# Splitting the masked queries of a two-stage attention kernel in three pieces of 512 columns in place of one of 1536

## The chip, the core and the metric

The kernel runs on one core of one Trainium2 chip. The metric is the time of one execution on the device in microseconds (us), the median of several runs. The engines are named as the profile names them: PE (TensorE, matmuls), PEld (its weight loads), DVE (VectorE), ACT (ScalarE), POOL (GpSimd) and SP (SyncE, which issues every DMA here).

## The reference

Two stages follow each other, for 8 batches `b`. In the first, 512 tokens and 32 state rows of 8 heads read each other by attention; this gives 576 rows of 512 columns. The second is a mixture of 4 attention experts of width 64, with 2 experts chosen for each token:

```python
logits = x @ w_gate                      # top 2 of 4 experts, softmax over the two: w
for e in range(E):
    q, k, v = x @ wq[e], x @ wk[e], x @ wv[e]
    scores = where(causal, -1e9, scale * (q @ k.T))
    ye = softmax(scores) @ v @ wo[e]
    out += (w of e where e was chosen) * ye
```

## The kernel before

**Numbers in two parts.** Matrix products run in f16, and an f32 operand is carried as a high part (rounded to f16) and a low part (what the rounding left). A product of two such operands is three matmuls: high by high, high by low, low by high (`PROD`). `split(n, hi, lo, src)` makes both parts of an f32 tile of n columns in two instructions. The high part is a copy that may run on ACT, POOL or DVE; the low part is the subtraction `src - hi`, which may run on POOL or DVE.

**The stages.** For each batch, `front(b)` loads x, splits it (`xh`, through the scaled copy `xn`), transposes it (`xT`), does the first stage's attention (`eb`, `at`), projects to keys (`kt`), values (`v`) and queries, and routes the tokens (`gate`). Then `probs(b, i)` and `reads(b, i)` run over 4 blocks `i` of 128 queries: scores, exponentials (`p`), their split (`ph`), a transposing DMA (`pt`), the product with the values (`z`), the output product and its store. Every second batch, `tail` does the state rows of two batches. `side` computes the state's reading of the tokens.

**The masked queries.** Only two of a token's four experts count, so the queries are folded: `projected(0, pr)` gives the queries of the expert pair `pr` in PSUM, and `mt[:, k]`, of three planes k of 512 columns, holds which tokens use which expert. Four DVE products write `qf` (f32, 128 x 3 x 512, one buffer): the first pair writes plane 0 and one half of plane 1 (64 partitions), the second pair plane 2 and the other half of plane 1. Plane 1 is therefore complete only with the last of the four, planes 0 and 2 before it. `split` then makes `qm` (f16, 128 x 2 x 3 x 512, two buffers), high and low. `probs` of every block reads all of `qm`: first planes 2 and 0 in all three products, high parts first, then the mask, then plane 1.

**The order of the work.** The kernel writes no order by hand. `Steps` collects every step with its duration, the views that it reads and writes and the engines that may run it (`either`), and derives from overlapping views which step waits for which. `plan` then places the steps one after the other, each at the engine where it would end first, with a bias against some engines: from batch 1 on `LEAN` adds 2.0 to DVE and 0.3 to ACT and POOL; for batch 0 `LEAN0` adds 0.3 to DVE and nothing to the others. It makes a DVE operation that shares POOL's access to SBUF (two SBUF inputs, for one) wait for POOL's current one. `run` repeats this over several rounds and then over 100 random changes of the steps' due times, and emits the best order that it has seen by its own estimate. All compute instructions are issued in one line, L447 of the profile, so groups are told apart by tiles.

Of the kernel before, what the change touches and what calls it, by code (L numbers as in the profile page):

```python
# [451 lines left out]
def state_read_then_moe_attention(ctx: ExitStack, tc: tile.TileContext, x, state, w_gate, wq, wk, wv, wo, out):  # L452
# [9 lines left out]
    B, H, S, D = x.shape  # L462
# [36 lines left out]
    def dve(n, f, **kw):  # L499
        st.do("DVE", 0.065 + n * 0.00104, f, **kw)  # L500
# [4 lines left out]
    def split(n, hi, lo, src):  # L505

        st.either([("ACT", 0.093 + n * 0.000833, (nc.scalar.activation, dict(out=hi, in_=src, func=AF.Copy, scale=1.0))),
                   ("POOL", 0.162 + n * 0.000832, (nc.gpsimd.tensor_scalar, dict(out=hi, in0=src, scalar1=1.0, scalar2=1.0, op0=ALU.mult, op1=ALU.mult))),
                   ("DVE", 0.065 + n * 0.00065, (nc.vector.tensor_copy, dict(out=hi, in_=src)))])
        kw = dict(out=lo, in0=src, in1=hi, op=ALU.subtract)  # L510
        st.either([("POOL", 0.147 + n * 0.001887, (nc.gpsimd.tensor_tensor, kw)), ("DVE", 0.065 + n * 0.00104, (nc.vector.tensor_tensor, kw))])
# [170 lines left out]
    def front(b):  # L682
# [126 lines left out]
        qm = st.buf("qm", [P, 2, 3, S], F16, bufs=2)  # L809
# [31 lines left out]
        qf = st.buf("qf", [P, 3, S], F32, bufs=CFG["qf"])  # L841
        for pr, h in (0, slice(D, P)), (1, slice(0, D)):
            pp = projected(0, pr)
            for r, k in (slice(0, P), 2 * pr), (h, 1):
                dve(S, nc.vector.tensor_tensor, out=qf[r, k], in0=pp[r], in1=mt[r, k], op=ALU.mult)
        split(3 * S, qm[:, 0].rearrange("p k s -> p (k s)"), qm[:, 1].rearrange("p k s -> p (k s)"), qf.rearrange("p k s -> p (k s)"))
        base = st.base
        st.stream("side", base + CFG["SIDE"], PACE * CFG["FSPAN"], 4.0)
        if b < CFG["PX"]:
# [276 lines left out]
    for b in range(B):  # L1126
        st.stream("front", (b - CFG["FRONT"]) * PACE, PACE * CFG["FSPAN"], 18.0)
        load(b, marks.get("w") if CFG["LB"] == 2 else None)
        front(b)
        st.stream("main", b * PACE, PACE, 16.0)  # L1130

        blocks = range(T) if b < B - 1 else range(T - 1, -1, -1)
        for k in range(T + LAG):
            if k < T:
                probs(b, blocks[k])
            if k >= LAG:
                reads(b, blocks[k - LAG])
        if b % NB == NB - 1:
            st.stream("tail", (b + CFG["TOFF"]) * PACE, PACE * CFG["TSPAN"], 8.0)
            tail(b // NB)  # L1140
# [29 lines left out]
```

## Time and profile before

| | us |
|---|---|
| time of 3 runs: median (lowest to highest) | 338.25 (337.67 to 338.3) |
| the profiled execution's own time | 337.99 |
| its span, first to last instruction | 336.2 |
| PE busy | 302.5 (90%) |
| DVE busy | 252.5 (75%) |
| POOL busy | 249.5 (74%) |
| ACT busy | 217.0 (65%) |

The span begins 0 at the first instruction. A row of a timeline gives start, duration, engine, operation, tiles and, in brackets, the idle time just before it and what ended it.

### The profile page before, as it was taken

Reading aid. Unit: us, or ns where it says so; the run is one execution under the profiler, and the core shown is the slowest. Engines: PE = TensorE matmul, PEld = TensorE weight load, DVE = VectorE, ACT = ScalarE, POOL = GpSimd, SP = SyncE. Lnnn points to the kernel's source line nnn. Section 1 sums busy time; section 2 is a strip of 40 time slices with the busy share of each in tenths; the row PEclk is TensorE's granted clock in tenths of the full one; section 3 lists DMA queues with packets and bytes.
Section 4 is the critical chain, followed back from the end, with each engine's and each line's share of the span. In section 5 each row is a group of like instructions: output and inputs, shape, how many; then the busy total and the mean of one; then the engine's idle time right before and its main releaser. Section 6 shows DMA issues by size and latency. Waiting matters only on the chain.

```text
span 336.2 us, 8884 instructions
## 1 busy us (share of the span) xinstructions
PE 302.5 (90%) x3274; PEld 198.5 (59%) x3274; DVE 252.5 (75%) x813; ACT 217.0 (65%) x481; POOL 249.5 (74%) x315
## 2 busy tenths in 40 slices
PE   6678698798897999999997999989999999999992
PEld 5445474584544776576664765467555876666750
DVE  4889969999988775998678656897679667775430
ACT  4686786585656975596688268665684867555431
POOL 8089497398988799999977999965996484485500
PEclk9999979999999899999999999999999999999998
DMA  8939649736788939989999795599696533357963
GB/s 195 216 98 204 169 96 183 164 62 121 104 171 111 208 80 189 190 192 201 195 169 168 162 202 96 79 179 167 137 154 128 111 64 69 72 97 133 142 155 98
DMA packets 142851, 48.16 MB, mean 143 GB/s; under 512 B 121816, under 2 KB 138200, under 8 KB 142808
## 3 DMA queue, kind: packets, MB, share of 16 engines
q1 hardware_dynamic: 142808, 47.61, 75.5%
q8 instruction: 25, 0.41, 0.5%
q14 instruction: 18, 0.15, 0.2%
HBM read 11.54 MB, written 8.91 MB: 61 GB/s over the span
## 4 chain that ended last, share of the span: by engine, by line
PE 37%; DVE 18%; POOL 15%; DMA 12%; ACT 11%; issue 5%; SPq 1%; ACTq 0%; POOLq 0%; DVEq 0%
PE bank L447 37%; DMA xn<-in_x_dram 3%; DMA pt<-ph 3%; POOL ph L447 3%; POOL xh L447 3%; DVE sbm L447 2%; DVE eb L447 2%; DVE m L447 2%; ACT e L447 2%; POOL at L447 2%; DVE qf L447 1%; DMA xT<-xh 1%; DMA p<-in_moe_wo_dram 1%; SPq L447 1%; POOL xn L447 1%
## 5 line engine op out<-in xcount | busy, mean ns | idle before, releaser
L447 PE MATMUL bank<-kt,qm 64*128 64x128 f16 (+7 forms) x384 | 50.0, 300 | 3.0 <-ACT p L447 1.4
L447 POOL TENSOR_TENSOR ph<-p,ph 128x256 f16<-128x256 f32 (+3 forms) x30 | 41.4, 1382 | 9.7 <-ACT ph L447 9.4
L447 PE MATMUL bank<-wo_n,z 128*128 128x512 f16 x192 | 47.0, 386 | 0.3 <-DMA z<-zh 0.3
L447 PE MATMUL bank<-v,pt 128*128 128x193 f16 x480 | 45.6, 249 | 0.7 <-DMA pt<-ph 0.7
L447 PE MATMUL bank<-at,gs 128*128 128x512 f16 x192 | 44.8, 380 | 0.5 <-DVE mx L447 0.5
L447 PEld LDWEIGHTS <-pt 128*128 128x128 f16 x480 | 40.9, 99 | 5.9 <-DMA pt<-ph 1.2
L447 ACT ACTIVATE p<-bank,mx 128x128 f32<-128x128 f32 (+3 forms) x64 | 31.5, 525 | 17.8 <-DVE mx L447 15.7
L447 POOL TENSOR_TENSOR xh<-xn,xh 128x512 f16<-128x512 f32 x28 | 33.8, 1207 | 2.3
L447 DVE TENSOR_REDUCE mx<-bank 128x1 f32<-128x128 f32 (+3 forms) x64 | 28.8, 480 | 8.7 <-PE bank L447 8.6
L447 ACT ACTIVATE o<-bank 128x512 f32<-128x512 f32 x34 | 20.2, 595 | 22.7 <-PE bank L447 22.7
L447 PE MATMUL bank<-gs,at 128*128 128x256 f16 (+1 forms) x384 | 31.2, 221 | 1.8 <-DVE at L447 1.0
L447 PEld LDWEIGHTS <-qm 64*128 64x128 f16 (+1 forms) x384 | 21.9, 96 | 18.4 <-issue 3.8
L447 PEld LDWEIGHTS <-z 128*128 128x128 f16 x192 | 17.8, 98 | 21.0 <-issue 2.6
L447 PEld LDWEIGHTS <-gs 128*128 128x128 f16 x192 | 17.5, 97 | 21.4 <-issue 3.1
L447 POOL TENSOR_TENSOR qm<-qf,qm 128x1536 f16<-128x1536 f32 x7 | 21.7, 3104 | 10.7 <-ACT qm L447 10.6
L447 PEld LDWEIGHTS <-at 128*128 128x128 f16 x384 | 24.1, 97 | 8.2 <-issue 1.9
L447 POOL TENSOR_TENSOR eb<-eb,sbm 128x512 f32<-128x512 f32 x16 | 16.7, 1049 | 12.8 <-DVE sbm L447 8.9
L447 DVE TENSOR_TENSOR qf<-bank,mt 128x512 f32<-128x512 f32 (+1 forms) x32 | 21.3, 683 | 3.6 <-ACT mt L447 1.7
L447 ACT ACTIVATE ph<-p 128x512 f16<-128x512 f32 (+3 forms) x28 | 21.1, 753 | 4.2 <-DMA pt<-ph 3.9
L447 ACT ACTIVATE xh<-xn 128x512 f16<-128x512 f32 x32 | 18.9, 625 | 5.7 <-DMA xn<-in_x_dram 4.9
L447 DVE SCALAR_TENSOR_TENSOR v<-bank,v 128x256 f16<-128x256 f32 x32 | 13.2, 420 | 10.2 <-ACT v L447 10.2
L447 PEld LDWEIGHTS <-bd 128*64 128x64 f16 x264 | 14.0, 109 | 11.4 <-issue 4.1
(170 smaller groups left out, 698.8 us busy)
## 6 DMA issues: line engine op xcount, KB each, us to landing
xn<-in_x_dram SPq DMA_DIRECT2D x16, 512.0 KB, 4.7
out_dram<-o SPq DMA_DIRECT2D x64, 128.0 KB, 2.5
sn<-in_state_dram SPq DMA_DIRECT2D x6, 128.0 KB, 2.8
p<-in_moe_wo_dram SPq DMA_DIRECT2D x2, 256.0 KB, 4.8
pt<-ph SPq DMA_TRANSPOSE x32, 4.0
out_dram<-o SPq DMA_DIRECT2D x2, 256.0 KB
z<-zh SPq DMA_TRANSPOSE x29, 2.9
xT<-xh SPq DMA_TRANSPOSE x28, 3.9
```

The lines of the kernel that those rows point to most:

```text
L447: f(**{k: v.ap() if isinstance(v, View) else v for k, v in kw.items()})
```

## The change

One call of `split` on all 1536 columns of `qf` becomes three calls on 512 columns, one for each plane k. So each batch has three high steps and three low steps, each of which waits only for the DVE products that write its plane, and each of which the planner may give to another engine. All else in the source is the same, and the planner makes the whole order anew.

```diff
-        split(3 * S, qm[:, 0].rearrange("p k s -> p (k s)"), qm[:, 1].rearrange("p k s -> p (k s)"), qf.rearrange("p k s -> p (k s)"))
+        for k in 0, 1, 2:
+            split(S, qm[:, 0, k], qm[:, 1, k], qf[:, k])
```

## Rows read from the trace of the kernel before

**Rows 1.** Busy us by stretch; columns: length, PE, PEld, DVE, ACT, POOL, clock, DMA, GB/s
```profile
40.00:50.00 10.00, 7.92 (x121) 6.40 (x121) 6.86 (x19) 8.94 (x19) 9.51 (x12) 0.83 0.37 76
50.00:60.00 10.00, 8.31 (x83) 4.55 (x82) 9.18 (x30) 6.61 (x17) 6.89 (x7) 1.00 1.05 177
60.00:70.00 10.00, 7.52 (x97) 4.88 (x94) 9.74 (x24) 5.98 (x14) 5.05 (x6) 1.00 0.55 120
70.00:80.00 10.00, 9.68 (x143) 8.05 (x141) 9.71 (x37) 7.56 (x18) 9.75 (x10) 1.00 0.70 134
80.00:90.00 10.00, 7.21 (x70) 3.50 (x69) 9.87 (x29) 5.82 (x15) 8.31 (x11) 1.00 0.48 92
...
107.00:137.00 30.00, 29.79 (x336) 20.84 (x337) 21.68 (x80) 23.12 (x55) 27.36 (x34) 0.94 0.80 160
...
245.00:310.00 65.00, 64.75 (x727) 43.08 (x728) 47.75 (x166) 41.97 (x91) 42.33 (x45) 1.00 0.54 104
```

**Rows 2.** Instructions of the tile qm: nanoseconds min/median/max, first and last start
```profile
L447 ACT ACTIVATE qm<-qf x7: 1467/1482/1484, 48.1 to 288.7; 128x1536 f16<-128x1536 f32 x7
L447 POOL TENSOR_TENSOR qm<-qf,qm x7: 3097/3106/3109, 75.5 to 290.3; 128x1536 f16<-128x1536 f32 x7
L447 DVE TENSOR_TENSOR qm<-qf,qm x1: 1949/1949/1949, 49.6 to 49.6; 128x1536 f16<-128x1536 f32 x1
L447 POOL TENSOR_SCALAR qm<-qf x1: 1464/1464/1464, 195.2 to 195.2; 128x1536 f16<-128x1536 f32 x1
```

**Rows 3.** Timeline of batch 0, 44 to 52 us
```profile
44.77 2.73 DVE L447 TENSOR_TENSOR qf<-bank,mt 128x512 f32<-128x512 f32 x4 [1.70 <-ACT mt L447]
...
48.06 1.48 ACT L447 ACTIVATE qm<-qf 128x1536 f16<-128x1536 f32 x1
48.17 1.16 POOL L447 TENSOR_TENSOR xh<-xn,xh 128x512 f16<-128x512 f32 x1
...
49.57 1.95 DVE L447 TENSOR_TENSOR qm<-qf,qm 128x1536 f16<-128x1536 f32 x1 [1.20 <-ACT qm L447]
...
50.00 2.54 POOL L447 TENSOR_TENSOR xh<-xn,xh 128x512 f16<-128x512 f32 x1
...
51.57 0.29 PE L447 MATMUL bank<-kt,qm 128*128 128x128 f16 x2 [1.21 <-DVE qm L447]
```

**Rows 4.** Timeline of batch 1, 71 to 79 us
```profile
71.43 2.01 DVE L447 TENSOR_TENSOR qf<-bank,mt 64x512 f32<-64x512 f32 x3
...
75.50 3.10 POOL L447 TENSOR_TENSOR qm<-qf,qm 128x1536 f16<-128x1536 f32 x1
...
78.66 0.28 PE L447 MATMUL bank<-kt,qm 128*128 128x128 f16 x2 [0.33 <-POOL qm L447]
```

**Rows 5.** Timeline of batch 2: its last part and its first score product
```profile
113.89 3.11 POOL L447 TENSOR_TENSOR qm<-qf,qm 128x1536 f16<-128x1536 f32 x1 [1.05 <-ACT qm L447]
...
119.14 0.51 PE L447 MATMUL bank<-kt,qm 128*128 128x128 f16 x6
```

**Rows 6.** Groups by shape: count, busy us, mean ns, idle before
```profile
L447 POOL TENSOR_TENSOR a<-e,a 128x512 f16<-128x512 f32 x14 | 16.2, 1156 | 1.2
L447 POOL TENSOR_SCALAR xn<-xn 128x512 f32<-128x512 f32 x28 | 18.7, 667 | 0.1
L447 DVE TENSOR_TENSOR ph<-p,ph 128x512 f16<-128x512 f32 x1 | 0.7, 693 | 0.4 <-ACT ph L447 0.4
L447 ACT ACTIVATE xh<-xn 128x512 f16<-128x512 f32 x32 | 18.9, 625 | 5.7 <-DMA xn<-in_x_dram 4.9 <-PE bank L447 0.7
```

**Rows 7.** Chain that ended last, around 195 us
```profile
194.34 0.87 POOL z L447 x2
195.21 1.45 POOL qm L447
...
198.18 4.29 DMA xn<-in_x_dram
```

**Rows 8.** Timeline, 145 to 147 us: a POOL and a DVE operation
```profile
145.83 1.05 POOL L447 TENSOR_TENSOR eb<-eb,sbm 128x512 f32<-128x512 f32 x1
145.94 0.96 DVE L447 TENSOR_SCALAR s<-s 128x2 f32<-128x2 f32 x1
```

**Rows 9.** Groups by shape: DVE's reciprocal of the two columns of s
```profile
L447 DVE RECIPROCAL s<-s 128x2 f32<-128x2 f32 x8 | 1.2, 156 | 0.1
```

**Rows 10.** Waits of all engines: who waited for whom, us, times, longest
```profile
PE bank L447 <- DVE xt_tail L447: 2.5, 1, 2.5
```

## The prediction

> **What bounds the kernel now.** I read the busy shares of the whole span first, then busy time by stretch, because an average over 336 us hides which engine is short where. Four stretches matter [rows 1]. From 107 to 137 us and from 245 to 310 PE is busy 29.79 of 30 and 64.75 of 65 us: nothing that makes an operand ready sooner can shorten these unless PE reaches them sooner. From 50 to 90 us it is DVE that is full: 9.18, 9.74, 9.71 and 9.87 of each 10 us, together 38.50 of 40, while PE does 8.31 + 7.52 + 9.68 + 7.21 = 32.72, so it idles 7.28. Between 40 and 50 POOL (9.51) and ACT (8.94) are the full ones. So time can be won ahead of 90 us, in the first two batches; what is won there is kept only if the nearly full engines behind it keep up, and POOL with 27.36 of 30 us from 107 on is the one to watch.
>
> Next I read the tile of the change. Each of the 8 batches has one high part of 1.48 us (7 on ACT, one on POOL of 1.46) and one low part (7 on POOL of 3.11, one on DVE of 1.95) [rows 2]. Then the timelines around them, to see how long PE stands for them. In batch 0 it waits 1.21 us for the DVE low part [rows 3], in batch 1 0.33 us for POOL's [rows 4]. In the others it doesn't: in batch 2 the low part ends at 113.89 + 3.11 = 117.00 and the first score product starts at 119.14 [rows 5], and none of the five later ones shows a wait of PE for qm.
>
> **The change part by part.** *Instructions and busy time.* Two instructions of 1536 columns become six of 512. ACT's copy of 512 columns costs 0.625, POOL's subtraction 1.156, DVE's 0.693, POOL's one-input operation 0.667 [rows 6]. Three of a kind against one: ACT 3 x 0.625 - 1.48 = +0.40, POOL's low part 3 x 1.156 - 3.11 = +0.36, DVE's 3 x 0.693 - 1.95 = +0.13, POOL's high part 3 x 0.667 - 1.46 = +0.54. With the engines of now that is 7 x 0.40 + 0.54 = 3.3 us of high parts and 7 x 0.36 + 0.13 = 2.7 us of low parts over the whole span. Nearly all of it falls where ACT or DVE have room; if all were on the path it would cost 6.0 us.
>
> The Trainium skill speaks on both sides here. Its page Perfetto Trace Analysis, section Optimizing Scalar/DVE Operations, says that each ScalarE or VectorE operation carries a fixed access overhead, so that larger operations pay on a saturated engine, and also that breaking up instructions may let work finish sooner where these engines are not saturated but leave bubbles on others. The rows agree with the first half as far as a fixed cost goes (+0.40 us on ACT). By the first half alone the time would rise by up to the 6.0 us; by the second, batch 0 gains. The sum below doesn't use the page.
>
> *Batch 0.* The four qf products run from 44.77 to 47.50. The one high part starts only at 48.06 and ends at 49.54; DVE stands 1.20 us for it, then makes the low part until 51.52; PE goes on at 51.57 after 1.21 us of idling [rows 3]. With three steps, plane 0 can be copied after the first product, and planes 0 and 2 need not wait for the last. DVE's 1.20 us of standing go, since the first low part needs a high part of 0.63 and not of 1.48 us, and two of these could be done before 48.06. DVE is the engine that is full for the next 40 us, so I count these 1.20 us as won. PE's own 1.21 us lie behind the same wait and are not counted a second time. Bounds: nothing, if ACT, full here, takes the copies no sooner than 48.06 and each low part waits for a free POOL; at most 47.50 + 0.63 + 0.69 = 48.82 in place of 51.52, 2.7 us. I take 1.2, what the rows call idle.
>
> *Batch 1.* The last qf product ends at 73.44, and the low part at 78.60, of which 3.10 are POOL's [rows 4]. Three pieces could end near 73.44 + 0.63 + 1.16 = 75.2, 3.4 us sooner, but PE waited only 0.33 us, with the key-side products filling the rest. I take 0.3; bounds 0 and 0.8, as DVE is full and sets when the next operands come.
>
> *Batches 2 to 7.* No wait of PE is removed, so no gain. The loss is on POOL. In the chain that ended last POOL runs almost alone around 195 us; the high part of batch 4 is in it with 1.45 us, ahead of the load of xn that the chain waits for next [rows 7]. If high and low stayed on POOL, this place would cost 0.54 + 0.36 = 0.9 us more. The planner can send single pieces to ACT or DVE, which it could not do with parts of one, so I take half, 0.4; bounds 0 and 0.9. The four other low parts, and the stores and loads that SP issues, I cost at nothing: PE's full queue covers them (64.75 of 65 us); without that cover they cost 0.36 us each.
>
> *Sum.* On the profiled execution: 337.99 - 1.2 - 0.3 + 0.4 = 336.9 us. The median of the runs is 338.25, 0.26 above that execution, so the forecast for a median is 337.15, rounded 337.1, 0.3% faster. A measurement of this kernel can tell about 0.2%, 0.7 us, from no change. By the bounds, all gains and no loss give 338.25 - 2.7 - 0.8 = 334.75; no gain and the loss of batch 4 give 339.15.
>
> **The rivals.** *The three DVE pieces wait three times for POOL (slower).* The trace shows that the two engines hold each other up. DVE's low part runs from 49.57 to 51.52, and POOL's xh, which starts at 50.00 and takes 1.16 us elsewhere, takes 2.54 [rows 3]. The other way round, DVE's scaling of two columns starts at 145.94 beside a POOL operation that ends at 146.88 and itself ends at 146.90, 0.96 us after its start [rows 8], where another operation on the same two columns takes 0.156 [rows 9]. In batch 0 POOL is busy without a break. One low part on DVE meets it once; three meet it up to three times. With 1.16 us for a POOL operation that has just begun and half of it, 0.58, on average, two further meetings cost 1.2 us, 2.3 at worst, on the engine that is full to 90 us. If that happens in batch 0 and again in batch 1, where a piece may go to DVE now, 2.4 us are lost on average and the gain of 1.5 is gone too, or partly: 338.25 + 2.4 - 0.5 = 340.2. It decides as soon as two or more pieces of the first batches are on DVE beside a POOL with no gaps. Against it: from batch 1 on the planner's bias of 2.0 keeps DVE from most pieces. The Trainium skill has this as a rule: its page SBUF — State Buffer, section SBUF: two separate sides, describes one port pair that DVE and GpSimd take in turn for a whole instruction, the other being blocked. Rows 3 and 8 agree with it.
>
> *The new order loses more than the pieces win (slower).* Every step is placed anew, and the search stops after a fixed number of rounds. What one badly placed step costs can be read from the waits: PE once stands 2.5 us for a low part of xt_tail [rows 10]. A second such wait ahead of a stretch in which PE is full, less the gain of 1.1, gives 338.25 + 2.5 - 1.1 = 339.65. For it speaks that PE has no slack to make it good after 107 us; against it, that a new order may as well lose the wait of now, which is the same 2.5 us the other way and part of why the range reaches below the sum.
>
> *Nothing comes of it (same).* DVE is full for 40 us behind batch 0. If the 1.20 us that it stood are filled with work that must then be done anyway, but PE's next operands still come at the old times, for instance because x arrives by DMA, the gain ends at 90 us: 338.25, at most 0.7 either way.
>
> **How the numbers follow.** The forecast (faster, most likely 337.1) has a chance of 0.43, with an own range from 334.8 to 337.5; nothing 0.19; three waits for POOL 0.20; the new order 0.18. Faster by over 0.2% is 0.43, within 0.2% 0.19, slower by over 0.2% 0.38. Cases of both signs are likely, so the range takes in both: down to 334.7 by the bounds, and up to 341.0, which is the first rival with its worst price in one batch and its average in the other, 338.25 + 2.3 + 1.2 - 0.5 = 341.25, cut slightly to leave out no more than 2 in 10 in all.
>
> **What would show it.** Right: ACT copies of 512 columns inside the run of the qf products in batch 0; DVE idle before its first low part under 0.3 us in place of 1.20; the first score product of batch 0 ahead of 51 us by a microsecond or more; PE idle between 40 and 90 us below the 2.08 + 7.28 us of now; and the later PE-full stretches as long as before but shifted forward. Wrong by the first rival: DVE low pieces of clearly more than 0.69 us, or POOL operations of 2 us beside them, before 90 us. Wrong by the second: a PE wait of 2 us or more that is not in the old list, on a tile that has nothing to do with the queries. Wrong by the third: batch 0 ahead, and the stretch that begins at 107 us where it was.

## The result, and the profile after

The changed kernel takes 333.84 us in the median (332.95 to 338.3, 4 runs; 332.95 to 334.33 without the highest) beside 337.96 of the kernel before (337.38 to 338.3): ratio 0.9872, 95% interval 0.9845 to 0.9898. Two later measurements gave 334.25 beside 337.24 (0.9925, 0.9883 to 0.9967) and 334.15 beside 337.52 (0.9889, 0.9852 to 0.9926). So it is faster by 0.8 to 1.3%, 3 to 4 us, where 1.1 us had been forecast, and the time lies just below the forecast range. One execution says less than I had assumed: 12 of the kernel before, timed beside the first of these later measurements, spread from 334.45 to 338.95 us.

The profile shown is of a second run of the changed kernel (334.44 us, span 332.2), because the first one that was taken (338.3 us) was disturbed. Busy time by stretch, columns as in [rows 1]:

```profile
40.00:50.00 10.00, 9.06 (x126) 6.31 (x125) 8.83 (x26) 8.91 (x22) 8.13 (x10) 1.00 0.31 28
50.00:60.00 10.00, 9.56 (x82) 5.29 (x81) 9.14 (x26) 7.81 (x17) 9.67 (x11) 1.00 1.03 158
60.00:70.00 10.00, 9.49 (x170) 7.69 (x168) 9.14 (x29) 5.67 (x16) 7.17 (x10) 1.00 1.14 204
70.00:80.00 10.00, 8.79 (x99) 6.57 (x97) 8.50 (x33) 6.91 (x18) 8.16 (x9) 1.00 0.96 171
80.00:90.00 10.00, 8.57 (x73) 4.57 (x73) 9.24 (x28) 7.32 (x16) 8.75 (x12) 1.00 0.81 170
107.00:137.00 30.00, 29.16 (x354) 18.70 (x352) 25.92 (x82) 23.86 (x57) 27.52 (x33) 1.00 0.60 122
```

PE is busy 45.47 of the 50 us from 40 to 90, where it was 40.64 [rows 1]: its idle time there fell from 9.36 to 4.53. That is where the forecast looked for the gain, and the amount is larger than forecast. (The clock of 0.83 in the first row of [rows 1] means that TensorE ran at 1.2 GHz in place of 2.4 for part of these 10 us; the changed kernel has such parts ahead of 40 and behind 90 us.) The timeline of batch 0 answers to [rows 3]:

```profile
38.33 1.55 ACT L447 ACTIVATE mt<-bank 128x512 bf16<-128x512 f32 x3
...
39.50 1.39 DVE L447 TENSOR_TENSOR qf<-bank,mt 64x512 f32<-64x512 f32 x2
...
40.93 0.63 ACT L447 ACTIVATE qm<-qf 128x512 f16<-128x512 f32 x1 [0.53 <-DVE qf L447]
...
41.63 2.35 POOL L447 TENSOR_TENSOR qm<-qf,qm 128x512 f16<-128x512 f32 x2 [0.38 <-ACT qm L447]
...
44.68 0.69 DVE L447 TENSOR_TENSOR qm<-qf,qm 128x512 f16<-128x512 f32 x1
44.79 0.39 PE L447 MATMUL bank<-kt,qm 128*128 128x128 f16 x4
45.43 0.28 PE L447 MATMUL bank<-kt,qm 128*128 128x128 f16 x2 [0.25 <-DVE qm L447]
```

The pieces stand between the qf products, as they should, and PE's wait for the last low part is 0.25 us where it was 1.21. But the row to look at is the one of qf: it starts at 39.50, not 44.77. Those 5.3 us are ahead of every instruction that the source change touches. The planner has put the whole front of batch 0 in another order; the masks `mt` are ready sooner, and everything behind them. So the profile alone leaves two readings open, the pieces or the order, and the experiments are there to part them.

The tile qm, as in [rows 2]:

```profile
L447 POOL TENSOR_TENSOR qm<-qf,qm x23: 1152/1157/1167, 41.6 to 285.5; 128x512 f16<-128x512 f32 x23
L447 ACT ACTIVATE qm<-qf x18: 614/630/653, 40.9 to 284.3; 128x512 f16<-128x512 f32 x18
L447 POOL TENSOR_SCALAR qm<-qf x6: 614/617/619, 44.0 to 257.2; 128x512 f16<-128x512 f32 x6
L447 DVE TENSOR_TENSOR qm<-qf,qm x1: 686/686/686, 44.7 to 44.7; 128x512 f16<-128x512 f32 x1
```

Prices are as forecast, POOL's high part a little cheaper (0.617 for 0.667), and the planner now spreads the high parts, 18 on ACT and 6 on POOL.

### The profile page after: what moved, and what is told of

The parts are those of the page before. It is cut to its first block, busy times and chain, and to the rows that moved or that the text cites. A ratio compares the mean times of both kernels' runs of the same rounds, so it can differ in the third digit from the quotient of the medians.

```text
span 336.0 us, 8909 instructions
## 1 busy us (share of the span) xinstructions
PE 307.3 (91%) x3274; PEld 200.0 (60%) x3274; DVE 252.7 (75%) x815; ACT 218.4 (65%) x498; POOL 250.2 (74%) x328
## 4 chain that ended last, share of the span: by engine, by line
PE 45%; DVE 22%; POOL 11%; DMA 11%; ACT 5%; issue 3%; SPq 1%; POOLq 0%; ACTq 0%
PE bank L447 45%; DMA xn<-in_x_dram 4%; POOL xh L447 3%; DMA pt<-ph 3%; DVE sbm L447 3%; DMA z<-zh 3%; POOL at L447 2%; POOL ph L447 2%; DVE qf L447 2%; DVE m L447 2%; DVE mx L447 2%; POOL xn L447 2%; DVE eb L447 2%; DVE gs L447 2%; DVE mb L447 1%
## 5 line engine op out<-in xcount | busy, mean ns | idle before, releaser
L447 PE MATMUL bank<-at,gs 128*128 128x512 f16 x192 | 46.3, 389 | 0.0
L447 PEld LDWEIGHTS <-pt 128*128 128x128 f16 x480 | 39.9, 98 | 7.7 <-DMA pt<-ph 3.1
L447 POOL TENSOR_TENSOR ph<-p,ph 128x256 f16<-128x256 f32 (+3 forms) x29 | 39.9, 1378 | 0.8 <-ACT ph L447 0.3
L447 PE MATMUL bank<-gs,at 128*128 128x4 f16 (+1 forms) x384 | 32.2, 223 | 3.9 <-DVE at L447 1.9
L447 POOL TENSOR_TENSOR xh<-xn,xh 128x512 f16<-128x512 f32 x28 | 32.5, 1160 | 2.3
L447 POOL TENSOR_TENSOR qm<-qf,qm 128x512 f16<-128x512 f32 x23 | 26.4, 1161 | 6.0 <-ACT qm L447 5.9
L447 POOL TENSOR_SCALAR xn<-xn 128x512 f32<-128x512 f32 x28 | 18.0, 643 | 14.1 <-ACT xh L447 12.5
L447 ACT ACTIVATE zh<-z 128x256 f16<-128x256 f32 x28 | 11.6, 416 | 17.5 <-POOL z L447 17.5
L447 DVE TENSOR_TENSOR qf<-bank,mt 64x512 f32<-64x512 f32 (+1 forms) x32 | 21.4, 683 | 2.0 <-ACT mt L447 1.5
L447 POOL TENSOR_TENSOR zh<-z,zh 128x256 f16<-128x256 f32 x29 | 19.9, 691 | 2.4 <-ACT zh L447 2.3
```

The lines of the kernel that those rows point to most:

```text
L447: f(**{k: v.ap() if isinstance(v, View) else v for k, v in kw.items()})
```

## The experiments

Theories, as they came: **A**, the pieces win by themselves, because the queries are ready sooner. **B**, the order wins, and the pieces only set off another search. **C**, the search makes orders for an assumed DMA landing time (`LANDS`: 1.4, 2.0 or 2.6 us behind a transfer) and keeps what it holds to be best; the order of the kernel before came from 2.0, that of the changed kernel from 2.6, and this decides. **D**, three pieces give better orders whatever the search assumes.

**E0. The changed kernel again**, for the profile above.

> The changed kernel itself once more, for a profile of an execution that is not disturbed. If its gain comes from the first batches (theory A: finer pieces make the masked queries of batch 0 ready sooner, and the time won there is kept), the time is 333 to 334.5 us, the first score product of batch 0 starts near 46 us in place of 49.98, and PE is 3 to 5 us ahead of the old order at every later batch. If it comes from a better order in the middle or at the end (theory B: the whole order is made anew, and the pieces are only what set off another search), PE is ahead by less than 2 us at 107 us and gets the rest later.

334.25 us. The first score product of batch 0 is at 44.79 us, 5.2 ahead. Those of batches 1 and 2 are at 76.22 and 116.91, 1.7 and 2.2 us ahead of 77.94 and 119.14, so the lead of batch 0 isn't kept one for one, and neither the 3 to 5 us of theory A nor the late gain of theory B is met.

```profile
76.22 0.51 PE L447 MATMUL bank<-kt,qm 128*128 128x128 f16 x6
...
116.91 0.51 PE L447 MATMUL bank<-kt,qm 128*128 128x128 f16 x6
```

**E1. The old order, three pieces in place.** One step still, so the planner sees nothing new; it issues three instructions (shortened; the low parts likewise).

```diff
-st.either([("ACT", 0.093 + n * 0.000833, (nc.scalar.activation, dict(out=hi, in_=src, ...))), ...
+st.either([("ACT", 0.093 + n * 0.000833, *[(nc.scalar.activation, dict(out=hi, in_=src, ...)) for hi, lo, src in q3]), ...
```

> The order of the kernel before, step by step and engine by engine; only at the place of each of the 16 steps that make qm stand three instructions of 512 columns on the same engine. Theory A (the pieces themselves win, by making the queries ready sooner): 335 to 336.5 us against 337.2 to 338 of the kernel before, PE's 1.21 us wait in batch 0 gone. Theory B (the order wins, the pieces only set off another search): within 0.3% of the kernel before, 336.5 to 338.5, since the pieces cost about 0.4 us a batch on POOL and ACT where these have room.

342.63 us, ratio 1.0146 (1.0091 to 1.0201): slower by about 5 us, above the ranges of both theories, and theory A falls in this form. Rows of batches 0, 1 and 4, and from near the end:

```profile
49.16 3.27 DVE L447 TENSOR_TENSOR qm<-qf,qm 128x512 f16<-128x512 f32 x3 [0.21 <-ACT qm L447]
49.31 1.56 POOL L447 TENSOR_TENSOR xh<-xn,xh 128x512 f16<-128x512 f32 x1
...
50.78 1.08 PE L447 MATMUL bank<-kt,qm 128*128 128x128 f16 x6
...
50.84 1.05 POOL L447 TENSOR_SCALAR xn<-xn 128x512 f32<-128x512 f32 x1
...
85.69 2.29 PE L447 MATMUL bank<-kt,qm 128*128 128x512 f16 x5 [1.41 <-ACT p L447]
...
204.71 0.50 PE L447 MATMUL bank<-kt,qm 128*128 128x128 f16 x6
...
304.82 2.00 DVE L447 TENSOR_SCALAR m<-twg 128x4 f16<-128x4 f32 x1
...
306.88 0.30 PE L447 MATMUL bank<-identh,m 128*64 128x128 f16 x4 [1.44 <-DVE m L447]
```

In batch 0 the pieces do what they were made for: DVE's idle time before its first low part falls from 1.20 to 0.21 us, and PE's wait of 1.21 us for the low part is gone. But DVE's three pieces take 3.27 us from first to last, not 3 x 0.693 = 2.08, and POOL's xh and xn beside them 1.56 and 1.05 where they take 1.16 and 0.62 elsewhere: the two engines take turns, as the first rival had it.

The loss comes later. PE runs the same matmuls in the same order in both kernels, so its lag can be followed. PE is 2.2 us behind at 64 us, but as it doesn't meet the wait of 2.5 us for xt_tail [rows 10], the first score product of batch 1 is 0.5 us ahead of the old one (77.44 against 77.94). From 84 to 91 us PE then ran mostly at 1.2 GHz; these are the stretches of E1 and of the kernel before:

```profile
84.00:91.00 7.00, 5.59 (x41) 2.07 (x41) 5.23 (x17) 4.43 (x12) 6.74 (x9) 0.53 0.58 110
```

```profile
84.00:91.00 7.00, 5.55 (x58) 3.15 (x57) 6.87 (x27) 4.95 (x14) 6.67 (x9) 1.00 0.59 113
...
86.06 1.24 PE L447 MATMUL bank<-kt,qm 128*128 128x512 f16 x5 [1.41 <-ACT p L447]
```

The same five products take 2.29 us for 1.24, and at 92 us PE is 2.0 us behind. PE had waited as long ahead of them in the kernel before, so why the clock fell in E1 alone isn't shown. At 107 us 1.7 us of the lag go again, when the kernel before has a stretch at 1.2 GHz of its own. Then come, among smaller ones, a wait of 0.91 us for POOL at 124.65 and, from 183 to 190, 2.1 us more (a longer wait for DVE, and a granted clock of 0.61 from 186 to 190). So the first score product of batch 4 is 4.0 us behind (204.71 against 200.71). At 306.88 PE waits 1.44 us for a DVE operation of 4 columns that took 2.00 us beside POOL, 0.17 in the kernel before, and the last score products are 5.4 behind (314.31 against 308.91). POOL's six pieces in batch 4 cost 0.75 us more than the two long steps, but PE's lag is 4.0 us before and behind them. These are the places of one execution, whose mean clock was 0.968; two others at 0.981 took 342.31 and 342.41 us, where two of the kernel before at 0.981 took 337.19 and 337.77. So the 5 us are not a matter of the mean clock. How they follow from the pieces, step by step, stays open.

**E2. The new order, one piece.** The changed kernel's order step by step; the three high parts are one instruction at the place of the last of them, and so the low parts.

```diff
+            calls = s["ways"][way][2]
+            if n in whole:  # a step of qm: nothing, or all 1536 columns at the last of three
+                calls = [whole[n][s["eng"]]] if whole[n] else []
```

> The order of the changed kernel, step by step; only the three high parts of a batch are one instruction of 1536 columns at the place of the last of the three, and so the three low parts. In batch 0 this makes the low part end about 2 us later (a high part of 1.46 on POOL, then a low part of 1.95 on DVE, in place of 0.62 and 0.68). Theory A: the gain is gone, 336.5 to 338.5 us. Theory B: most of the gain stays, 333.5 to 336 us, and the values and logits of batch 0 are as early as in the changed kernel.

338.77 us, ratio to the kernel before 1.0032 (0.9992 to 1.0072): the whole gain is gone, so theory B falls as well. Timeline rows of PE in batches 0, 1 and 2:

```profile
46.60 0.29 PE L529 MATMUL bank<-kt,qm 128*128 128x128 f16 x2 [1.40 <-DVE qm L529]
...
78.82 0.28 PE L529 MATMUL bank<-kt,qm 128*128 128x128 f16 x2 [0.99 <-POOL qm L529]
...
120.54 0.28 PE L529 MATMUL bank<-kt,qm 128*128 128x128 f16 x2 [1.19 <-POOL qm L529]
```

PE now stands 1.40 + 0.99 + 1.19 = 3.58 us for low parts, against 0.25 with pieces. The front is as early as in the changed kernel (qf at 39.35). So the new order has no room for the long steps: what the pieces save there is a wait of PE of about 3.3 us, of the 4.6 us between the two. PE runs the same matmuls in the same order here as in the changed kernel, and behind the third wait its lag is 3.4 us.

**E3, E4. Other seeds** of the search (`random.Random(1)`): the kernel before with 5, the changed kernel with 2.

> The kernel before with the seed of its 100 random changes set to 5 in place of 1; the low and high parts in one step of 1536 as before. Theory A: the search finds about as good an order, 337 to 338.5 us. Theory B: orders differ by a per cent for no reason in the source, so 333 to 340 us, and more than 1 us away from the kernel before is likely.

> The changed kernel with the seed 2 in place of 1. Theory A: the gain of the pieces stays, 333 to 335 us. Theory B: another draw of an order, 334 to 340 us, with the gain of the change halved or gone.

339.11 us (1.0040, 1.0003 to 1.0077) and 332.67 (0.9849, 0.978 to 0.9918). Both are other orders than those of seed 1, and yet the sides stay as they were. Both searches again ended at 2.0 us for one piece and at 2.6 for three, hence theory C. That could not be otherwise: `run` goes through the landing times before it draws its first random number, and the random changes keep the one that was best. A seed alters only the last 100 changes to the same starting order.

**E5 to E12. Landing time and pieces crossed**, up to three seeds each.

```diff
-    LANDS = (1.4, 2.0, 2.6)
+    LANDS = (2.0,)   # or (2.6,)
```

> The changed kernel, but the search may use only one of its three assumed DMA landing times, 2.0 us, from which the order of the kernel before came; the order of the changed kernel came from 2.6 us. Theory C (the change only tipped the search to orders made for slower DMAs, which suit the chip better): 336.5 to 340 us, the gain gone. Theory D (three pieces give the search better orders, whatever it assumes): 332 to 335 us. Theory B (any order is a draw): no telling, 332 to 341.

> As the run before, with seed 2. Theory C: 336.5 to 340 us. Theory D: 332 to 335. Theory B: far from the run before in either direction, by more than 2 us.

> The kernel before, steps of 1536 columns, its search held to a landing time of 2.6 us. Theory C: 332.5 to 335.5 us, the gain without the pieces. Theory D: 337 to 340 us. Theory B: 332 to 341.

> As the run before, with seed 2. Theory C: 332.5 to 335.5 us. Theory D: 337 to 340. Theory B: more than 2 us away from the run before.

> Third seed, three pieces, landing time 2.6 us. If the landing time that the search assumes decides (theory C), about 332.5 to 336 us, below both orders of this seed made for 2.0 us. If the orders are draws (theory B), anywhere in 332 to 341.

> Third seed, one piece, landing time 2.6 us. Theory C alone: as the run with three pieces, within 1 us. If the pieces help once the landing time is right (theory C with a smaller share for the pieces), 335 to 337.5 us, 2 to 3 us above the run with three pieces. Theory B: 332 to 341.

> Third seed, three pieces, landing time 2.0 us. Theory C: 338 to 342 us, slower than the kernel before. Theory B: 332 to 341.

> Third seed, one piece, landing time 2.0 us. Theory C: 336.5 to 340 us, as the kernel before. Theory B: 332 to 341.

**E13, E16, E17. A longer landing time**, `LANDS = (3.2,)`.

> Three pieces, the search held to a landing time of 3.2 us, longer than any that the kernel lets it assume. If orders made for slower DMAs are better because they leave room for transfers that come late (theory C), 332.5 to 335.5 us, as at 2.6; if 2.6 is only a lucky value, 336 us or more.

> One piece, landing time 3.2 us, seed 2. If the trend with the landing time holds without the pieces too, 333.5 to 336 us; if one piece has no room left to fill longer assumed transfers, 336.5 us or more, and the pieces are what lets the order use them.

> Three pieces, landing time 3.2 us, seed 2, a second draw beside the 332.3 us of seed 1: 331.5 to 334 us if the trend is real, 335 or more if the first was a lucky order.

All medians in us; the order of E4 gave 334.09 when it was timed again (E14); the kernel before, timed beside each, had 337.2 to 338.0:

| landing time assumed | one piece | three pieces |
|---|---|---|
| 2.0 | 337.5 (before), 339.11 (E3), 339.58 (E12) | 339.59 (E5), 341.68 (E6), 340.65 (E11) |
| 2.6 | 336.43 (E7), 336.05 (E8), 335.29 (E10) | 334.25 (changed), 332.67 (E4), 333.29 (E9) |
| 3.2 | 339.88 (E16) | 332.27 (E13), 329.50 (E17) |

Means: one piece 338.7, 335.9, 339.9; three pieces 340.6, 333.4, 330.9. By their medians all six orders made for 2.6 us are faster than all six made for 2.0, but with one piece only E10 is clear of the kernel before (0.9899 to 0.9966; E7 0.9925 to 1.0008, E8 0.995 to 1.0025). E7 and E8 lie between what C and D expected, and E6 lies 2.1 us from E5, which only B expected. At 2.0 the pieces cost 1.9 us, at 2.6 they win 2.5, at 3.2 some 9. So theory D falls (at 2.0 three pieces lose), and theory C alone does not do either: for one piece 3.2 is worse than 2.6 (E16). In this table the gain needs pieces and landing time together. Whether the assumed time itself is the cause is not shown: the seeds of one field share their starting order, so the table compares six starting orders and not fifteen, and that each of the six is a draw of its own (theory B for the starting orders) was not tested. E17 at 329.50 us, ratio 0.9803 (0.9731 to 0.9876), beats the kernel before and, by its median, the changed one.

What the chip does with it can be seen in part in PE's waits for DMAs. From the waits of E6, three pieces at 2.0, and of E17, three pieces at 3.2 (who waited for what: us, times, longest):

```profile
PE bank L447 <- DMA pt<-ph: 2.5, 3, 1.4
PE bank L447 <- DMA p<-in_moe_wv_dram: 2.2, 1, 2.2
PE bank L447 <- DMA xT<-xh: 1.5, 1, 1.5
PE bank L447 <- DMA z<-zh: 1.5, 1, 1.5
```

```profile
PE bank L447 <- DMA pt<-ph: 2.2, 2, 1.1
PE bank L447 <- DMA sn<-in_state_dram: 0.5, 1, 0.5
PE bank L447 <- DMA p<-in_moe_wv_dram: 0.4, 1, 0.4
```

Such waits sum to 9.6, 7.7 and 11.7 us for three pieces at 2.0 (E5, E6, E11) and to 3.8, 8.5 and 5.4 at 2.6 (E0, E4, E9); for one piece to 6.1, 4.3 and 6.7 at 2.0 and to 4.7, 3.0 and 4.9 at 2.6. The direction fits and the size doesn't: E4, at 332.67 us the fastest of the three at 2.6, waits 8.5, and E13, at 332.27, 7.8.

**E14, E15. The order of seed 2 beside the changed kernel.**

> The fastest order so far (three pieces, seed 2, landing time 2.6 us) once more, beside the changed kernel on the same chip: 332 to 334 us and 0.5 to 1.5 us below the changed kernel if it is really the better order, the same within 0.7 us if both are draws of one kind.

> The changed kernel itself, timed beside the order of seed 2 on the same chip: 333.5 to 335 us, as in its run before this one, whichever theory holds.

334.09 and 334.15 us: no difference, though the order of seed 2 had given 332.67 in E4. So medians of one order, taken at different times, differ by up to 1.4 us here.

## Why the prediction was right in direction and wrong in size

**The sum was made in the wrong order of work.** The step that failed is the sum over batches 0, 1 and 4 (-1.2 - 0.3 + 0.4), with the rest and the new order at nothing: each price was read at the place that the step had in the old order. E1 comes nearest to that sum, the old order with three pieces on the old engines, and it is about 5 us slower, not 1.1 faster. What the sum counted as won does show in batch 0: DVE idles 0.21 us for 1.20, and PE's 1.21 us are gone. But this time isn't kept. DVE spends it on turns with POOL (3.27 us for the three pieces, 1.95 for the one), and PE loses more later, at places that the sum had at nothing (2.4 us from 80 to 92, 1.5 at 306). The first rival's mechanism is thus shown where its condition holds, in E1, with 1.3 us of DVE's time where it had 1.2 on average; the changed kernel escapes it since only one low piece is on DVE.

**Batches 2 to 7: "no wait is removed, so no gain".** True for the old order, where 2.1 us lay between batch 2's low part and its first product [rows 5]. In the new order there is no such room, and in E2 PE stands 1.19 us there. The old order had been made with the long step in it; that the room was there for this reason is argued, not shown.

**The new order** was taken only as a rival that loses, with the remark that it might win as well. It is where the gain came from, but only together with the pieces: each half alone loses it (E1, E2). The lower end of the range had no term for it; its 334.7 is made of the bounds of the pieces alone. The forecast of PE idling less ahead of 90 us held (4.53 for 9.36 us), and so did the products coming sooner; both are the work of the order and the pieces together, and the 5.3 us by which qf is early are the order's alone.

**What a measurement can tell.** The forecast took 0.2%. The intervals of single comparisons here are 0.27 to 0.73% to each side.

**How much is chance.** Which landing time a search ends with is its own pick among three, and the forecast could not know it: with the change it went from 2.0 to 2.6, and holding it at 2.0 turns the gain into a loss of 0.6 to 1.5% (E5, E6, E11). So the direction was luck in part. Of the 3 to 4 us, the table gives about 1.6 to the other starting order without pieces (337.5 to 335.9, clear of noise in one of three orders) and 2.5 to the pieces at 2.6 us. Each field holds one to three orders from one start, so these shares are rough. Why one piece gets worse again at 3.2 us, in a single order, was not followed further; it is what one would see too if each starting order were a draw of its own.

## What to carry to other kernels

Where a search makes the order, the price of a smaller step can't be read at its old place: in E1 the time that the shorter steps won was not kept in the old order, and in E2 the new order had no room for the long ones. Run both halves, new pieces in the old order and old pieces in the new order, before giving the gain to either. And look at what the search assumes of late transfers: here the orders made under three such assumptions lay further apart (340.6, 333.4 and 330.9 us on average with three pieces) than the kernels before and after the edit. But ask first how many starting orders stand behind such a comparison: a new seed that only alters the last changes isn't a new draw.

## What the runs showed of the hardware that was not expected

VectorE and GpSimd working on SBUF operands take turns instruction by instruction: in E1 three DVE subtractions of 512 columns, 0.69 us for the one in the changed kernel, took 0.69 to 1.64 us each and 3.27 from first to last, beside POOL operations that grew from 1.16 to 1.56 and from 0.62 to 1.05. One of 1536 columns took 1.95 us in the kernel before and 1.76 in E2. Cutting a DVE operation beside a busy POOL thus cost 1.3 us of DVE's time there.

A DVE operation that writes only 4 columns was held too: it took 2.00 us in E1 (304.82 to 306.82) beside POOL's low part of ph that began at 304.67 and takes 2.13 us elsewhere, and 0.17 us in the kernel before.
